# Three chained blocks on one core: the weight range check, the place of the rms gain, the first loads and the written order

## The chip, the cores and the metric

The kernel runs on one core of one Trainium2 chip. The metric is the device time of one execution in microseconds (us). The kernel before took 1032.06 us (median of 3 runs, 1030.85 to 1033.56). Engines are named as in the profile: PE is TensorE, DVE is VectorE, ACT is ScalarE, POOL is GpSimd, SP is SyncE, which issues the DMAs.

## The reference, cut to what matters

Three stages follow one another. The first is a linear recurrence over 768 positions for 4 batches of 8 heads of width 48, with complex decays normalised to a magnitude of at most 0.999. Its output becomes a matrix x of 3072 rows and 384 columns.

```python
new_re = ar * S_re - ai * S_im          # every position t, every head
new_im = ar * S_im + ai * S_re
S_re, S_im = new_re + k[t] (outer) v[t], new_im
y[t] = q[t] @ S_re
...
xn = x / rms(x) * rms_g                 # stage 2: 384 -> 1536 -> 384
x = (silu(xn @ w_gate) * (xn @ w_val)) @ w_out
h = max(x @ w1, x @ w2, x @ w3)         # stage 3: 384 -> 768 -> 384
out = h @ w_out2
```

The weights and `rms_g` arrive as 64-bit floats; the kernel reads them as pairs of 32-bit words.

## The kernel before, in words

**Two versions, one flag.** `fast` computes everything under assumptions about the ranges of the data; `ok_flag` (from line 1324) tests the assumptions, and `general` runs afterwards only if a test fails. With the inputs here only `fast` runs.

**Precision.** Every weight and every activation of stages 2 and 3 is split into two 16-bit floats, high and low, and a product is three matmuls: high by high, high by low, low by high (`mm3`, lines 1134 to 1137).

**Streams.** The work is cut into named steps. `x0` to `x11` are twelve pieces of the recurrence (two batches by 128 positions each): loads, squares (`sq0`, `sq1`), minima (`m20`, `m21`), logarithm and norm, a scan of 7 levels on DVE (`scan1x` to `scan7z`), small complex products (`pre`), the scaled q and k (`pa`, `qh`, `kr`, `kh`), transposes on PE (`tq`, `tk`), score products (`qk`), a triangular mask on POOL (`msk`), value products (`pv`), the state update (`kv`, `wa`, `wd`, `wu`), the row norm (`rs`), and the transposed, split result: `yt` on PE, then `xh` and `xl` into the tiles XH and XL. `m0` to `m5` are six blocks of 512 rows of stages 2 and 3: gate and value products (`g`, `v`), `silu`, `gate`, the split `uh`, `ul`, the product with `w_out` (`acc`, `last`), `fh`, `fl`, then stage 3: `h00` to `h52`, maxima (`mx`), split (`hh`, `hl`), `om` and the store (`ob`, `od`). Blocks 0 and 1 do stage 2 in two pieces of 256 rows (`m0`, `m0b`, `m1`, `m1b`); the others in one piece.

**Weights.** `c0` to `c59` turn the 64-bit weights into the pairs: 60 tiles of 128 by 384, each with a load (384 KB on SP's queue, three buffers), `low` on ACT (line 427), `join` and `sign` on DVE (lines 432, 436), `high` (a scaled cast, line 440) and `rest`, the remainder. For the first 24 tiles (`BYPE`) the remainder is made on PE (`dif`, lines 444 and 445: the tile times a scaled diagonal matrix `down`, minus the high part) and cast from there; for the other 36 it is one DVE instruction.

**Range test of the weights.** `norms` (lines 479 to 496) forms, for 16 groups of weights, the products of the high part with itself: `nmm` on PE (line 489, 180 matmuls of 128 columns in all) and `nmax` on DVE (line 493), which takes the largest entry off the diagonal into `g_w`. `ok_flag` compares `g_w` with limits. `late` loads all 60 weight tiles again near the end and reduces them to smallest and largest magnitudes per row, `g_low` and `g_top` (lines 469 and 473).

**The rms gain** is loaded to `gts` (line 388), clipped on DVE (`gcl`, line 391), and multiplied in when the transposed rows are split: `xh` does three scaled casts and `xl` three DVE instructions for each half of a piece (from lines 1016 and 1023), one per 128 columns, because the gain differs in each.

**Order.** Nothing is scheduled by a program at run time: `ORDER` is a string of 3682 step names, written out, and `emit` issues the steps in that order. Each engine takes its own instructions in that order, so the string fixes five queues. A name with `/a`, `/v` or `/p` also says which engine does that step (ACT, DVE, POOL). In the order before, 393 steps stand ahead of the first gate product of block 0 (`m0.g0`), 775 ahead of that of its second piece (`m0b.g0`), 1137 ahead of the fourth group of stage 3 of block 0 (`m0.h30`) and 1226 ahead of the first gate product of block 1 (`m1.g0`).

Of the kernel before, what the change touches and what calls it, by code (L numbers as in the profile page):

```python
# [32 lines left out]
BYPE = range(0, 24)  # L33
# [5 lines left out]
SW, SX, SU, S1, SH = 2.0 ** 10, 2.0 ** 8, 2.0, 2.0 ** 2, 2.0 ** 2  # L39
# [214 lines left out]
def fast(  # L254
# [148 lines left out]
    for f in (con, eye, off, tri, sels, diag, one, zero, ld_g, gcl):  # L403
        at("k", -20.0, f"k.{f.__name__}", f)
# [8 lines left out]
    def conv(t, dst, r, c0, src, r0):  # L413
# [25 lines left out]
        def high():  # L439
            mv(dst[0][:, r, c0:c0 + CW], L["c"].bitcast(F32), -SW * 2.0 ** -128)  # L440

        def dif():
# [4 lines left out]
        def rest():
# [31 lines left out]
    def norms(t, dst, rows, c0, slot):  # L479
        n = len(jobs) - 1  # L480
        L = {}

        def nmm():
            p = pm.tile([128, 3, 128], F32, tag="m", name="nrm")
            L["p"] = p
            for j in range(3):
                w = dst[0][:, :, c0 + 128 * j:c0 + 128 * j + 128]
                for r in range(rows):
                    nc.tensor.matmul(p[:, j, :], lhsT=w[:, r, :], rhs=w[:, r, :], start=(r == 0), stop=(r == rows - 1))

        def nmax():
            junk = xp.tile([128, 3, 128], F32, tag="junk", name="junk")
            nc.vector.tensor_tensor_reduce(out=junk, in0=L["p"], in1=offd.to_broadcast([128, 3, 128]), scale=1.0,  # L493
                                           scalar=-1e30, op0=ALU.add, op1=ALU.max, accum_out=g_w[:, slot:slot + 1])
        at("c", t(n + 3.0), f"n{slot}.nmm", nmm)
        at("c", t(n + 3.0), f"n{slot}.nmax", nmax)

# [1208 lines left out]
```

## Time and profile before

| | |
|---|---|
| runs before | 1030.85, 1032.06, 1033.56 us |
| profiled execution | 1028.46 us, its span 1026.7 us |
| mean granted TensorE clock | 0.983 of full speed |
| PE busy | 956.3 us, 93% of the span |
| DVE busy | 818.5 us, 80% |
| ACT busy | 478.0 us, 47% |
| POOL busy | 66.6 us, 6% |
| HBM traffic | 70.78 MB read, 4.72 MB written |

The span runs from the first to the last instruction; the execution's time is 1.8 us longer. "Busy" for PE is the union of matmuls whose ends are modelled, so it is an upper view of the work. Times inside the profile are counted from the start of the span.

### The profile page before, as it was taken

Reading aid. Unit: us, or ns where it says so; the run is one execution under the profiler, and the core shown is the slowest. Engines: PE = TensorE matmul, PEld = TensorE weight load, DVE = VectorE, ACT = ScalarE, POOL = GpSimd, SP = SyncE. Lnnn points to the kernel's source line nnn. Section 1 sums busy time; section 2 is a strip of 40 time slices with the busy share of each in tenths; the row PEclk is TensorE's granted clock in tenths of the full one; section 3 lists DMA queues with packets and bytes.
Section 4 is the critical chain, followed back from the end, with each engine's and each line's share of the span. In section 5 each row is a group of like instructions: output and inputs, shape, how many; then the busy total and the mean of one; then the engine's idle time right before and its main releaser. Section 6 shows DMA issues by size and latency. Waiting matters only on the chain.

```text
span 1026.7 us, 17237 instructions
## 1 busy us (share of the span) xinstructions
PE 956.3 (93%) x6409; PEld 602.0 (59%) x6409; DVE 818.5 (80%) x2025; ACT 478.0 (47%) x939; POOL 66.6 (6%) x67
## 2 busy tenths in 40 slices
PE   2686898998999999999999999999999999999997
PEld 1364776855688975654655555656455555544443
DVE  5999999997965899849889568998648899985261
ACT  5677677764562565514563325474225351211100
POOL 1010030021000011000101000101001000000000
PEclk9888998999999999999999999999999999999999
DMA  7464563641321133121221131213011426682001
GB/s 193 144 174 116 137 181 92 189 124 27 69 72 28 38 69 70 39 53 49 51 51 34 22 74 44 51 44 77 1 45 52 116 87 193 212 279 78 1 1 34
DMA packets 84652, 87.52 MB, mean 85 GB/s; under 512 B 51920, under 2 KB 69200, under 8 KB 84560
## 3 DMA queue, kind: packets, MB, share of 16 engines
q1 hardware_dynamic: 84560, 86.34, 30.9%
q8 instruction: 52, 0.85, 0.3%
q14 instruction: 40, 0.33, 0.1%
HBM read 70.78 MB, written 4.72 MB: 74 GB/s over the span
## 4 chain that ended last, share of the span: by engine, by line
PE 62%; DVE 10%; DMA 2%; ACT 2%; issue 2%; POOL 1%; SPq 1%; DVEq 0%; ACTq 0%; POOLq 0%
PE gv L1135 7%; PE gv L1136 7%; PE gv L1137 7%; PE hm L1135 5%; PE hm L1136 5%; PE hm L1137 5%; PE acc L1135 3%; PE acc L1136 3%; PE acc L1137 3%; PE yp L897 3%; PE tp L838 2%; PE qk L862 2%; PE om L1289 2%; PE om L1291 2%; PE om L1290 2%; PE kp L943 2%
## 5 line engine op out<-in xcount | busy, mean ns | idle before, releaser
L880 POOL TENSOR_SCALAR_AFFINE_SELECT P<-P 128x512 f32<-128x512 f32 x48 | 62.1, 1304 | 794.1 <-ACT P L332 739.4
L1135 PE MATMUL gv<-XH,wgh 128*128 128x256 f16 (+1 forms) x288 | 94.5, 328 | 3.5 <-DVE g_w L493 1.9
L1135 PE MATMUL gv<-XH,wvh 128*128 128x256 f16 (+1 forms) x288 | 94.7, 329 | 3.2 <-ACT sg L1163 3.2
L1136 PE MATMUL gv<-XL,wgh 128*128 128x256 f16 (+1 forms) x288 | 94.4, 328 | 1.9 <-DVE XL L267 1.9
L1137 PE MATMUL gv<-XH,wgl 128*128 128x256 f16 (+1 forms) x288 | 94.4, 328 | 1.1 <-DVE wgl L267 1.1
L1137 PE MATMUL acc<-uh,wol 128*128 128x256 f16 (+1 forms) x288 | 93.8, 326 | 1.0 <-DVE wol L267 1.0
L1137 PE MATMUL gv<-XH,wvl 128*128 128x256 f16 (+1 forms) x288 | 94.7, 329 | 0.0
L1136 PE MATMUL gv<-XL,wvh 128*128 128x256 f16 (+1 forms) x288 | 94.7, 329 | 0.0
L1135 PE MATMUL acc<-uh,woh 128*128 128x256 f16 (+1 forms) x288 | 93.9, 326 | 0.0
L1136 PE MATMUL acc<-ul,woh 128*128 128x256 f16 (+1 forms) x288 | 93.8, 326 | 0.0
L1163 ACT ACTIVATE sg<-gv 128x256 f32<-128x256 f32 (+1 forms) x96 | 46.4, 489 | 84.3 <-PE gv L1137 71.8
L267 DVE SCALAR_TENSOR_TENSOR sg<-gv,sg 128x256 f32<-128x256 f32 (+1 forms) x96 | 52.8, 552 | 33.0 <-PE gv L1137 31.8
L267 DVE SCALAR_TENSOR_TENSOR hs<-hm,hs 128x512 f32<-128x512 f32 x72 | 49.4, 687 | 31.7 <-PE hm L1137 31.2
L343 DVE TENSOR_TENSOR ul<-sg,uh 128x256 f16<-128x256 f32 (+1 forms) x96 | 53.2, 559 | 14.5 <-ACT uh L332 13.9
L332 ACT CAST uh<-sg 128x256 f16<-128x256 f32 (+1 forms) x74 | 36.3, 495 | 57.9 <-DVE sg L267 35.3
L862 PEld LDWEIGHTS qk<-qT,kT 96*128 96x128 f32 x384 | 48.4, 196 | 3.9 <-issue 0.8
L862 PE MATMUL qk<-qT,kT 96*128 96x128 f32 x384 | 50.3, 281 | 0.0
L1289 PE MATMUL om<-uoh,HH 128*128 128x384 f16 x144 | 47.0, 326 | 0.0
L1291 PE MATMUL om<-uoh,HL 128*128 128x384 f16 x144 | 46.9, 326 | 0.0
L1290 PE MATMUL om<-uol,HH 128*128 128x384 f16 x144 | 46.9, 326 | 0.0
L354 ACT ACT_TABLE_LOAD x34 | 43.6, 1283 | 1.4 <-PEq L1690 0.8
L897 PE MATMUL yp<-P,v 128*64 128x128 f32 x384 | 35.8, 275 | 7.6 <-POOL P L880 7.5
(231 smaller groups left out, 2322.0 us busy)
## 6 DMA issues: line engine op xcount, KB each, us to landing
kn<-KH SPq DMA_DIRECT2D x160, 48.0 KB
raw<-in_moe_w_out_dram SPq DMA_DIRECT2D x18, 384.0 KB
raw<-in_moe_w_dram SPq DMA_DIRECT2D x18, 384.0 KB
lw<-in_moe_w_out_dram SPq DMA_DIRECT2D x18, 384.0 KB
lw<-in_moe_w_dram SPq DMA_DIRECT2D x18, 384.0 KB
ar<-in_a_re_dram SPq DMA_DIRECT2D x24, 192.0 KB
ai<-in_a_im_dram SPq DMA_DIRECT2D x24, 192.0 KB
raw<-in_moe_w_gate_dram SPq DMA_DIRECT2D x12, 384.0 KB
```

The lines of the kernel that those rows point to most:

```text
L267: nc.vector.scalar_tensor_tensor(out=o, in0=a, scalar=s, in1=b, op0=op0, op1=op1)
L343: eng[on(opts)].tensor_tensor(out=o, in0=a, in1=b, op=op)
L862: nc.tensor.matmul(p[:, j, :], lhsT=kT[:, h, :], rhs=qT[0:96, h, :], start=True, stop=True)
L880: nc.gpsimd.affine_select(out=P, in_=P, pattern=[[0, 4], [1, TP], [TP, TQ]], base=0, channel_multiplier=-1, compare_op=ALU.is_ge, fill=0.0)
L897: nc.tensor.matmul(L["y", jb][64 * z:64 * z + 64, 2 * g + pair, :], lhsT=(vt if part else Wf)[:, c:c + 64], rhs=P[:, 2 * pair + z, :] if p ...
L1135: nc.tensor.matmul(o, lhsT=wh, rhs=xh, start=first, stop=False)
L1136: nc.tensor.matmul(o, lhsT=wh, rhs=xl, start=False, stop=False)
L1137: nc.tensor.matmul(o, lhsT=wl, rhs=xh, start=False, stop=last)
L1163: nc.scalar.activation(s, L.pop(("g", j)), AF.Silu, scale=1.0 / (SW * SX))
L1289: nc.tensor.matmul(p, lhsT=hh[:, j, ts], rhs=WO2[0][:, j, :], start=(j == 0), stop=False)
L1290: nc.tensor.matmul(p, lhsT=hh[:, j, ts], rhs=WO2[1][:, j, :], start=False, stop=False)
L1291: nc.tensor.matmul(p, lhsT=hl[:, j, ts], rhs=WO2[0][:, j, :], start=False, stop=(j == NJ2 - 1))
```

## The change

The test by products goes; in its place `ok_flag` derives bounds from the row maxima that `late` already gathers. The gain `rms_g` is multiplied into the rows of `w_gate` and `w_val` when they are converted (`gsc` holds gain times scale, and `down` becomes one diagonal per group of 128 rows), so `xh` and `xl` become one instruction each on 384 columns. The first `ai` load is issued from ACT's queue beside `ar` on SP's. The 24 tiles whose remainder is made on PE are now the gate and value tiles among the first 36. The constants `offd` and `mask` go. Two power-of-two scales change (SU, SH). The order is written anew: 3649 steps, with 36 activation-table changes where there were 34; 349 steps stand ahead of `m0.g0`, 745 ahead of `m0b.g0`, 1078 ahead of `m0.h30` and 1186 ahead of `m1.g0`. The 16 `nmm` and 16 `nmax` are gone from it.

```diff
-BYPE = range(0, 24)
+BYPE = [n for n in range(36) if n % 9 < 6]
...
     def diag():
-        nc.scalar.mul(down, ident, -SW * 2.0 ** -128)
+        for kt in range(KT):
+            nc.scalar.mul(down[:, kt], ident, gsc[:, kt:kt + 1])
         nc.scalar.mul(less, ident, -1.0)
...
     def gcl():
         nc.vector.tensor_scalar(out=gts, in0=gts, scalar1=5.9, scalar2=-5.9, op0=ALU.min, op1=ALU.max)
+        nc.vector.tensor_scalar(out=gsc, in0=gts, scalar1=-SW * 2.0 ** -128, scalar2=None, op0=ALU.mult)
...
+        by = gsc[:, r:r + 1] if gain else -SW * 2.0 ** -128
...
         def high():
-            mv(dst[0][:, r, c0:c0 + CW], L["c"].bitcast(F32), -SW * 2.0 ** -128)
+            mv(dst[0][:, r, c0:c0 + CW], L["c"].bitcast(F32), by)
...
-    def norms(t, dst, rows, c0, slot):
...
-                    nc.sync.dma_start(out=t[:, jb].rearrange("p t d -> p (t d)"),
+                    dma = nc.scalar if n == 0 and nm == "ai" else nc.sync
+                    dma.dma_start(out=t[:, jb].rearrange("p t d -> p (t d)"),
...
         def xh(jb):
-                for kk in range(KT):
-                    mv(XH[:, kk, c0:c0 + 128], L["yT", jb][:, kk], gts[:, kk:kk + 1])
+                mv(XH[:, :, c0:c0 + 128], L["yT", jb])
...
         def xl(jb):
-                for kk in range(KT):
-                    stt(XL[:, kk, c0:c0 + 128], L["yT", jb][:, kk], gts[:, kk:kk + 1], XH[:, kk, c0:c0 + 128],
-                        ALU.mult, ALU.subtract)
+                tt(XL[:, :, c0:c0 + 128], L.pop(("yT", jb)), XH[:, :, c0:c0 + 128], ALU.subtract)
...
     def ok_flag():
-        ge(o[4], g_w, 0.5 * SW * SW)
-        tt(o[5], g_w, lim, ALU.is_le)
...
+        nc.vector.memset(ones, 1.0)
+        t = top[:, :NW]
+        nc.vector.tensor_scalar(out=t.bitcast(I32), in0=g_top.bitcast(I32), scalar1=3, scalar2=None,
+                                op0=ALU.logical_shift_left)
+        nc.vector.tensor_scalar(out=t, in0=t, scalar1=-2.0 ** -128, scalar2=None, op0=ALU.mult)
+        ge(o[8], t, 2.0 ** -6)
+        tt(t, t, t, ALU.mult)
+        p = pat.tile([128, NW // 3, 3], F32, tag="p", name="pn")
+        nc.tensor.matmul(p.rearrange("p t r -> p (t r)"), lhsT=ones, rhs=t, start=True, stop=True)
+        nc.vector.tensor_reduce(out=o[9], in_=p, axis=mybir.AxisListType.X, op=ALU.add)
+        le(o[9], o[9], 12.0)
...
 ORDER = """
-k.con k.eye x0.ld_ar k.one k.diag k.zero k.sels x0.ld_ai c0.load c4.load c2.load k.tri x0.ld_v0 k.off x0.ld_q x0.sq0/a
-x0.ld_k x0.ld_v1 x0.sq1/a k.ld_g x0.m21 x0.m20 c0.low c0.join x0.ln c0.sign c0.high/v c0.dif c1.load c4.low x0.nt0
...
+k.con x0.ld_ai k.eye x0.ld_ar k.tab k.one k.zero k.sels c0.load c14.load c10.load x0.ld_v0 k.ld_g x0.sq1/v x0.ld_k
+x0.ld_v1 x0.ld_q x0.sq0/a x0.m20 x0.m21 c0.low x0.ln c0.join c0.sign c4.load c14.low x0.nt0 c14.join c14.sign c10.low
...
```

In the new order, between `m0b.g0` and `m1.g0`, the last conversions come before most of `x3`'s scan, and eight of `x3`'s wide products (`pa`, `qh`) and its `n21` and last `pre` steps, which stood ahead of `m1.g0`, stand behind it.

## Rows read from the trace of the kernel before

**Rows 1.** The page, part 1: busy time, share of span, instructions.
```profile
PE 956.3 (93%) x6409; PEld 602.0 (59%) x6409; DVE 818.5 (80%) x2025; ACT 478.0 (47%) x939; POOL 66.6 (6%) x67
```
**Rows 2.** Windows: stretch, length, busy of PE, PEld, DVE, ACT, POOL; clock, DMA share, GB/s.
```profile
86.50:160.20 73.70, 60.79 (x558) 51.10 (x558) 71.00 (x196) 54.47 (x123) 8.15 (x4) 0.98 0.46 129
160.20:204.60 44.40, 41.56 (x368) 36.22 (x368) 43.77 (x101) 32.43 (x68) 0.00 (x0) 0.93 0.50 146
204.60:243.40 38.80, 33.57 (x233) 21.22 (x233) 33.71 (x75) 20.76 (x42) 9.24 (x4) 0.96 0.36 93
243.40:263.40 20.00, 19.83 (x100) 9.59 (x99) 19.42 (x65) 11.34 (x25) 0.00 (x0) 1.00 0.08 19
263.40:1019.30 755.90, 748.00 (x4880) 452.06 (x4877) 578.55 (x1394) 299.49 (x560) 40.32 (x36) 1.00 0.26 68
```
**Rows 3.** Timeline of PE at m0b.g0, m0.h30 and m1.g0: start, length, instruction.
```profile
160.21 0.37 PE L1135 MATMUL gv<-XH,wgh 128*128 128x256 f16 x1 [0.46 <-ACT XH L334]
...
162.19 0.42 PE L1135 MATMUL gv<-XH,wgh 128*128 128x256 f16 x1
...
243.44 0.38 PE L1135 MATMUL hm<-X1H,u0h 128*128 128x512 f16 x1
...
263.39 0.27 PE L1135 MATMUL gv<-XH,wgh 128*128 128x256 f16 x1
```
**Rows 4.** Windows of tile nrm alone: stretch, length, PE and DVE busy; clock, DMA.
```profile
0.00:243.40 243.40, 10.77 (x135) 6.59 (x12) 0.94 0.52 144
243.40:1027.00 783.60, 2.84 (x45) 2.20 (x4) 1.00 0.25 67
```
**Rows 5.** Groups by form: nmax, XL, XH, one 384-column cast, one 768-column product.
```profile
L493 DVE CUSTOM_DVE_ANT_1 junk<-nrm,offd 128x384 f32<-128x384 f32 x16 | 8.8, 550 | 0.1
L267 DVE SCALAR_TENSOR_TENSOR XL<-yT,gts,XH 128x128 f16<-128x128 f32 x72 | 20.2, 344 | 6.7 <-ACT XH L334 6.7
L334 ACT ACTIVATE XH<-yT,gts 128x128 f16<-128x128 f32 x60 | 17.1, 373 | 10.7 <-PE yT L1012 10.6
L332 ACT CAST wgl<-dif 128x384 f16<-128x384 f32 x9 | 4.3, 476 | 2.8 <-PE dif L445 2.7
L343 DVE TENSOR_TENSOR QH<-AA,q 128x768 f32<-128x768 f32 x24 | 22.4, 950 | 0.0
```
**Rows 6.** Timeline of DVE: two instructions that do not wait for each other.
```profile
26.05 0.35 DVE L264 TENSOR_TENSOR m<-AA 128x192 f32<-128x192 f32 x1
26.32 0.35 DVE L264 TENSOR_TENSOR m<-AA,ar 128x192 f32<-128x192 f32 x1
```
**Rows 7.** Timeline of the opening, all engines.
```profile
0.81 1.47 SPq L561 DMA_DIRECT2D ar<-in_a_re_dram  x2
2.33 1.24 SPq L561 DMA_DIRECT2D ai<-in_a_im_dram  x2
5.81 0.84 ACT L348 ACTIVATE Zn<-ar 128x768 f32<-128x768 f32 x1 [2.48 <-DMA ar<-in_a_re_dram]
9.32 0.84 ACT L348 ACTIVATE Rn<-ai 128x768 f32<-128x768 f32 x1 [2.67 <-DMA ai<-in_a_im_dram]
10.19 0.56 DVE L586 CUSTOM_DVE_ANT_0 Zn<-Zn,Rn 128x384 f32<-128x384 f32 x1 [9.22 <-ACT Rn L348]
11.99 1.30 SPq L388 DMA_DIRECT2D gts<-in_moe_rms_g_dram  x1
20.71 0.16 DVE L391 TENSOR_SCALAR gts<-gts 128x3 f32<-128x3 f32 x1
```
**Rows 8.** Timeline near the flag: the transpose of its minimum.
```profile
993.78 0.27 PE L1355 MATMUL pf<-ident,lo 128*1 128x128 f32 x1 [0.78 <-DVE lo L1353]
```
**Rows 9.** Waits of DVE, 200 to 260 us: the longest one.
```profile
DVE uol L267 <- ACT uoh L334: 4.8, 1, 4.8
```
**Rows 10.** Windows again: two stretches with both engines nearly full.
```profile
154.00:180.00 26.00, 21.52 (x183) 17.86 (x181) 25.32 (x75) 20.22 (x44) 0.00 (x0) 0.87 0.33 93
359.00:411.00 52.00, 48.62 (x398) 34.98 (x397) 49.57 (x125) 31.12 (x62) 9.29 (x6) 1.00 0.34 70
```

More of the change, by code (lines that the diff above doesn't have):

```diff
@@ L401, in zero @@
             nc.gpsimd.memset(z[96:128], 0.0)
-    for f in (con, eye, off, tri, sels, diag, one, zero, ld_g, gcl):
+    for f in (con, tab, eye, sels, ld_g, gcl, diag, one, zero):
         at("k", -20.0, f"k.{f.__name__}", f)
@@ L477, in late @@
             at("l", t, f"l{n}.{f.__name__}", f)
-    def norms(t, dst, rows, c0, slot):
[L480 to L496, printed above, removed]
     def ctime(n):
@@ L1444 @@
-c28.rest c32.load c24.high/a m0.gate8 x1.tq00 x1.ck01/a x2.ai x1.cq00/a c24.rest m0.acc6 m0.uh8/a x2.aim m0.ul8
-x1.qk01 x3.ld_ai x2.ain/a x2.ar c27.low x1.qk00 n5.nmax x2.ar0/a x1.qkc01/a c27.join c31.low x2.scan1x x1.tq10
-x1.msk01 c27.sign x1.qkc00/a c31.join x1.cq10/a c25.load x1.tq11 x1.msk00 x2.scan1y c32.low c31.sign x1.tk10
-c27.high/a x2.scan1z c33.load c31.high/a x2.scan2x n6.nmm c27.rest x1.ck10/a m0.g9 c31.rest x1.cq11/a c32.join
-x3.sq1/a x1.tk11 x2.scan2y c32.sign x1.pv00 x1.ck11/a x2.scan2z c26.load x1.pv01 n6.nmax c32.high/a n7.nmm x2.scan3y
@@ L1474 @@
-m0b.ul9 m0b.g11 c52.sign m0b.gate10 c51.load c52.high/a c56.join m0b.v11 m0b.uh10/a c52.rest m0b.silu11 m0b.ul10
-m0b.acc8 m0b.gate11 c53.low c56.sign m0b.acc9 c53.join c48.load m0b.uh11/a c56.high/a x1.wu1z m0b.acc10 m0b.ul11
-c56.rest c51.low c53.sign m0b.last0 c51.join m0b.last2 c46.load c53.high/a x2.pw x1.msm c51.sign m0b.fh0/a m0b.fh2/a
-m0b.last1 m0b.fl0 c45.load c51.high/a n9.nmm m0b.fl2 c48.low c53.rest n10.nmm m0b.fh1/a c51.rest n13.nmm x2.t12
-m0b.fl1 c48.join n10.nmax x2.rc c48.sign m0.h00 n9.nmax c59.load n13.nmax c48.high/a x2.kr0x c46.low x2.kr1x m0.h01
@@ new lines @@
+x0.ld_v1 x0.ld_q x0.sq0/a x0.m20 x0.m21 c0.low x0.ln c0.join c0.sign c4.load c14.low x0.nt0 c14.join c14.sign c10.low
+x0.nt1 c9.load k.gcl x0.nu c0.high/a c14.high/a x0.nt2/a k.diag x0.ai c0.dif x0.aim c10.join c14.dif x0.ain/a x1.ld_ai
+x0.ar c0.rest/a c10.sign x0.ar0/a x0.scan1y c14.rest/a c2.load x0.scan1x c10.high/a c10.dif x0.scan1z x0.scan2x
+x0.scan2y c10.rest/v x0.scan2z c4.low x0.scan3y x0.scan3x c4.join x0.scan3z c4.sign c9.low x0.scan4y c5.load x0.scan4x
+c4.high/a c4.dif c9.join x0.scan4z c9.sign x0.scan5y c9.high/a c3.load c9.dif x0.scan5x c4.rest/a x0.scan5z x1.sq1/a
@@ new lines @@
+x1.tk11 m0.gate8 x1.pw c28.low x2.scan5x x2.scan5y m0.uh8/a c28.join x1.ck11/a m0.ul8 x1.t12 x1.pv00 x2.scan5z
+c28.sign x1.pv01 x2.scan6y c28.high/a x1.qk10 c31.load x2.scan6x x1.yu0/a x2.scan6z c28.dif x2.scan7x x3.sq1/a
+x2.scan7y x3.ld_ar x2.scan7z x1.qkc10/a x1.yb0 c27.low x2.pt x1.msk10 x1.yc0/a c27.join x2.ptc x1.qk11 c27.sign
+c29.low x2.pre0x c32.load x1.pv10 x2.pre0y c27.high/a c29.join c27.dif x1.qkc11/a x2.pre1x c29.sign x1.ssq0/a x1.kv0
+x1.msk11 x2.pre1y c31.low c25.load x2.pre2x c27.rest/a x2.pre2y x2.pre2z c31.join c29.high/a c29.dif x2.pre3x
@@ new lines @@
+c54.sign m0b.fh0/a m0b.last2 c52.low m0b.fl0 c45.load m0b.fh1/a c52.join m0b.fh2/a c54.high/a m0b.fl1 m0b.fl2 m0.h00
+c59.low c52.sign c54.rest c52.high/a c56.load m0.h01 c59.join m0.mx00/a c52.rest c59.sign c45.low c57.load m0.h02
+c59.high/a c45.join m0.mx01 c59.rest c56.low c45.sign m0.h10 m0.mx02 c45.high/a c58.load c56.join c45.rest c57.low
+c56.sign m0.h11 m0.mx10/a c57.join c46.load c56.high/a c57.sign c56.rest c57.high/a c47.load m0.h12 c57.rest c58.low
+m0.mx11 c58.join c58.sign m0.h20 x2.rc m0.mx12 c58.high/v c58.rest x3.ln m0.h21 x2.kr0x x2.kr1x x2.kr0y x2.kr1y
@@ new lines @@
+c47.low x2.kr0z m0.h22 c46.low x2.kr1z x2.kh0 x3.ld_k x2.kh1 x2.tk00 x2.kn0 c47.join x2.ck00/a x2.tk01 c46.join
+x2.ck01/a c47.sign x3.nt0 x2.qk01 c46.sign c47.high/a x3.nt1 x2.qk00 x2.qkc01/a c46.high/v x2.msk01 x3.nu x2.tk10
+x2.qkc00/a x2.ck10/a x2.tk11 c46.rest x2.msk00 x3.nt2/v x2.kn1 x2.pv00 x2.ck11/a c47.rest swap m0.hh0/a x3.ai m0.hh1/a
+x2.pv01 m0.hl0 x2.tq10 x3.ar x2.yu0/a x2.cq10/a x2.tq11 x3.aim x2.yb0 x2.cq11/a m0.hl1 x2.yc0/a x2.kv0 x3.ain/a
+m0.big0 x4.ld_ai x2.ssq0/a x3.ar0/v x2.qk10 x3.scan1y m0.mx20/a x3.scan1x x3.ld_v0 x2.wa0 m0.h30 x3.scan1z x2.wd0
```

576 lines of the change are left out of this document (273 added, 303 removed).

## The prediction, made before the result was known

> **What bounds the kernel now.** I read the busy shares first: PE 93%, DVE 80% [rows 1]. An average over a kernel with two regimes says little, so the windows come next, and in them I looked for which engine has no idle time [rows 2]. From 86.5 to 204.6 us DVE is busy 71.00 of 73.7 and 43.77 of 44.4 us, PE 60.79 and 41.56: VectorE sets the pace, because it converts the weights beside three pieces of the recurrence. From 263.4 us to the last product PE is busy 748.0 of 755.9 us and DVE only 578.55: TensorE sets it. Between 204.6 and 263.4 one hands over to the other. So the time is: the opening, plus the DVE work that stands ahead of the hand-over in the order, plus the PE work that stands behind it, plus small waits. I take `m1.g0`, at 263.39 us [rows 3], as the marker; 763.3 us lie behind it (1026.7 less 263.4). All other waits named in the profile (ACT, POOL) are of engines that neither bounds.
>
> How DVE work is counted: an instruction of a queue that is full costs its length less about 0.08 us, since the next starts before it ends (0.35 us long, 0.27 apart [rows 6]). I went down both orders to the marker and summed by kind of step. Only the differences matter.
>
> **Part 1, the norm products go.** DVE loses 12 `nmax` ahead of the marker, 6.59 us busy by their windows [rows 4]; at 0.55 less 0.08 and the read-out behind each, 12 x 0.53 = 6.4 us. The four others (2.20 us) lie where DVE has slack: nothing. PE loses 10.77 us ahead of 243.4, where DVE sets the pace: nothing by themselves, and 2.84 us behind it, where PE is full: a whole gain.
>
> **Part 2, one `xh` and one `xl`.** Three XL instructions of 0.344 [rows 5] cost 3 x 0.26 = 0.78 us. One on 384 columns is not in the trace; a 384-column DVE instruction that reads PSUM is the `nmax`, 0.55, so 0.47 net and 0.31 us saved. Bounds: net 0.26 (as for 128 columns) to 0.78 (no gain). For the six pairs ahead of the marker 1.9 us, between 0 and 3.1; the 18 pairs behind it fall where DVE has slack. `xh`: three of 0.373 on ACT become one like the 384-column cast, 0.476: 24 x 0.6 = 15 us of ACT, on an engine 47% busy: nothing; if ACT were the late one, it would be a further gain.
>
> **Part 3, engine changes in the new order.** Counting the suffixes ahead of the marker, DVE takes over two squares, two `cq`, one `qkc`, two `ys`, two `uh`, one `high`, one `rest`, one `ar0` (from 0.88 us for a 768-column square, a width that takes 0.95 [rows 5], down to 0.13) and gives up a `yc`: together 5.0 us more. What it frees on ACT is covered.
>
> **Part 4, moved steps.** Eight 768-column products of `x3` (`pa`, `qh`; 0.950 less 0.08 each [rows 5], 7.0 us) and 1.2 us of its small steps go behind the marker, where DVE has 177 us of slack in all (755.9 less 578.55 [rows 2]); three `wu` and one `hl` come ahead, 2.0 us. Cost if that cover fails is the same 6 us. On PE two `tq` and one `pb`, about 1.1 us, go behind the marker and count there. SP's queue: its loads are reordered, but each conversion's load still finds its buffer freed by the third load before it, 4 us of DVE work or more ahead of its use but for one at 2 us, and the order before has tighter ones; I charge nothing. Two more table changes on ACT: covered.
>
> **Sum to here.** DVE ahead of the marker: -6.4 -1.9 +5.0 -8.2 +2.0 = -9.5 us. PE behind it: -2.84 +1.1 = -1.7 us. Together -11.2. The same count at `m0.h30` (243.44 us [rows 3]) gives -11.3 for DVE and +1.1 for PE, -10.2, because other steps are moved past that point. I take -10.5.
>
> **Part 5, the opening.** The first DVE work of size starts at 10.19 us, after `ai`'s square; `ar` is there at 5.81, `ai` at 9.32 [rows 7]. In the new order both are issued in parallel and squared on two engines. Bounds: nothing (the data moves no sooner) and 3.5 us (`ai` as early as `ar`). The two share the engines, so I put `ai` at about 7.6, the middle, and the square of `sq1` on DVE costs 0.1 more: -2.0 us after rounding up for the square that no longer waits behind another on ACT. [...] The new `diag` and every gate or val `high` wait for the gain. Its load is issued some eight issues earlier than now (11.99 us, used at 20.71 without a wait [rows 7]), `gcl` stands behind about 4 us of DVE work, at 12 to 13 us, so nothing; at worst, if landing takes the whole 8.7 us from issue to use, 1 to 2 us once. Four small casts for `diag` instead of two on ACT and the dropped POOL constants: covered by ACT's 2.5 us of waiting for `ar`.
>
> **Part 6, the flag.** PE now waits 0.78 us for the minimum [rows 8]. The new flag adds a product with a matrix of ones in PE's queue, and a DVE sum, a comparison and the minimum between it and the old transpose, so PE, with block 5's products queued behind, waits a second time. Bounds: 0 and 2.5; about 0.3 for the product and 1.0 for the hand-over back, so +1.3 us.
>
> **Result.** -10.5 -2.0 +1.3 = -11.2 us on a span of 1026.7. The profiled execution (1028.46) lies 3.6 us under the median of the runs; from the median, 1032.06 - 11.2 = **1021 us**.
>
> **Rivals.** (a) *The wait inside the hand-over goes as well.* In 200 to 260 us DVE waits 4.8 us once, for a cast behind a queue of ACT [rows 9]. In the new order the last conversions stand ahead of the late score copies that ACT was held by. If nothing takes its place: 1032.06 - 11.2 - 4.8 = 1016, with the full 3.5 us in the opening 1015. For: the order at that place; against: PE's new work between `h22` and `h30` is a chain of transposes, scores and masks with almost no other product between, so a similar wait can sit there.
>
> (b) *Lockstep.* In the new order PE's and DVE's work from `m0b.g0` to `m1.g0` are nearly equal (85 and 87 us, before 88 and 96). Two full in-order queues that feed each other lose time on both. In 359 to 411 us, where both are nearly full, PE idles 3.4 of 52 us [rows 10]; on 85 us that is 6 us more. 1027; with no gain in the opening 1029, and the change is not worth telling from noise. About 3 us, 0.3%, is what a measurement of this kernel can tell from none.
>
> (c) *Slower: the idle share of 154 to 180 us becomes the rule.* There DVE is full and PE idles 4.5 of 26 us, 17% [rows 10]. From `m0b.g0` to block 1's `h00`, the new order has 203 us of PE work and 194 of DVE, where the old had 201 and 182, so DVE is late more easily right after the marker. Before, PE idles 8.2 us from 160.2 to the marker [rows 2] and 3.4 more by the end of block 1's gate products [rows 10], 12 in all; at 17% it would idle 42, 30 more: 1051. It decides once some 23 us, 10% of the stretch, are lost. Speaking against: in 263 to 1019 us PE idles 7.9 us in all [rows 2]. [...]
>
> (d) *The second queue does nothing* for `ai`: 1023; it is inside the range of the forecast and changes no sign.
>
> **How the numbers follow.** Forecast with its bounds (1016 to 1028): 0.55. (a), below 1016: 0.14. (b), 1029 to 1035: 0.15. (c), above 1035: 0.16. Faster by over 0.3% (under 1029): 0.69; within 0.3%: 0.15; slower: 0.16. Range: the low end is (a) with the full opening and 4 us off the small waits, 1011; the high end is (b) plus the flag's upper bound and a late gain, 1033, which leaves most of (c) outside.
>
> **What would show each step.** The rows of `nrm` gone; XL and XH in 24 instructions each, near 0.55 and 0.48; the first DVE minimum at about 8 us instead of 10.19; `m0.h30` near 231 and `m1.g0` near 252 us; DVE full until about 230 us; PE idle of about 8 us from there to the last product; a second PE wait near the flag of about 1 us. The prediction is wrong if `m1.g0` comes at 260 or later (the DVE count or the opening failed), or if PE's idle time behind it exceeds 15 us (a new wait in the order), and wrong the other way if DVE's long wait goes and `m1.g0` comes before 248.

## The result, and the profile after

The kernel after takes **1018.78 us** (median of 4 runs, 1017.69 to 1019.02) against 1032.81 for the kernel before in the same session (4 runs): ratio 0.9863, 95% interval 0.9843 to 0.9883. That is 14.0 us less, 2.2 us under the forecast of 1021 and inside its range. The profiled execution took 1017.69 us (span 1016.0), 10.7 us less in span than that of before; the sum of the prediction was 11.2. Of these 10.7, 8.2 lie ahead of `m1.g0` and 2.5 behind it.

The page of the kernel after, part 1 [answers to rows 1]:

```profile
PE 941.9 (93%) x6231; PEld 589.8 (58%) x6231; DVE 818.4 (81%) x1966; ACT 462.5 (46%) x877; POOL 60.9 (6%) x63
```

The shares are those of before, so they say nothing of the cause. The windows between the same steps do [rows 2]; in order: `m0.g0` to `m0b.g0`, to `m0.h00`, to `m0.h30`, to `m1.g0`, to near the end.

```profile
85.65:164.19 78.54, 66.05 (x519) 51.22 (x518) 76.56 (x194) 57.56 (x121) 4.49 (x4) 0.96 0.50 136
164.19:202.07 37.88, 37.29 (x344) 33.21 (x341) 36.31 (x86) 25.48 (x63) 0.00 (x0) 1.00 0.62 179
202.07:232.78 30.71, 28.37 (x183) 16.54 (x181) 29.79 (x57) 22.48 (x41) 2.72 (x2) 1.00 0.47 118
232.78:255.21 22.43, 22.43 (x141) 11.99 (x139) 22.00 (x78) 11.10 (x22) 2.48 (x2) 1.00 0.18 50
255.21:1008.60 753.39, 746.15 (x4846) 450.56 (x4844) 584.68 (x1369) 293.32 (x526) 41.99 (x36) 1.00 0.25 69
```

`m0b.g0` comes 4.0 us later than in the profile before, `m0.h00` 2.5 earlier, `m0.h30` 10.7 earlier, `m1.g0` 8.2 earlier [rows 3]. From `m0b.g0` to `m1.g0` PE and DVE are each busy 88.1 of 91.0 us: the two are nearly full together. Behind the marker, up to the end of the last window, PE idles 7.2 us (7.9 before). PE's timeline at the three steps:

```profile
164.19 0.27 PE L1100 MATMUL gv<-XH,wgh 128*128 128x256 f16 x1
...
232.78 0.38 PE L1100 MATMUL hm<-X1H,u0h 128*128 128x512 f16 x1
...
255.21 0.27 PE L1100 MATMUL gv<-XH,wgh 128*128 128x256 f16 x1
```

The groups [rows 5]: `nrm` is gone, and XL and XH have the lengths that were forecast (0.55 and 0.48).

```profile
L264 DVE TENSOR_TENSOR XL<-yT,XH 128x384 f16<-128x384 f32 x24 | 12.6, 550 | 0.7 <-ACT XH L330 0.7
L330 ACT CAST XH<-yT 128x384 f16<-128x384 f32 x19 | 8.7, 477 | 2.9 <-PE yT L981 2.9
```

DVE's waits from 200 to 260 us: where before one of 4.8 us stood [rows 9], the longest is now

```profile
DVE HL L341 <- ACT HH L330: 0.5, 1, 0.5
```

The opening [rows 7] went the other way than forecast: the first minimum starts at 12.11 us, not at 8, and not at 10.19 as before.

```profile
0.82 1.86 ACTq L533 DMA_DIRECT2D ai<-in_a_im_dram  x2
0.82 1.53 SPq L533 DMA_DIRECT2D ar<-in_a_re_dram  x2
2.40 0.45 SPq L402 DMA_DIRECT2D raw<-in_moe_w_gate_dram  x1
...
8.94 0.84 ACT L346 ACTIVATE Zn<-ar 128x768 f32<-128x768 f32 x1 [4.40 <-DMA ar<-in_a_re_dram]
...
11.00 0.96 DVE L348 TENSOR_TENSOR Rn<-ai 128x768 f32<-128x768 f32 x1 [10.01 <-DMA ai<-in_a_im_dram]
12.11 0.56 DVE L558 CUSTOM_DVE_ANT_0 Zn<-Zn,Rn 128x384 f32<-128x384 f32 x1
```

PE at the flag [rows 8]: two waits, 2.45 us lost between the product at 980.47 and the one at 983.14 (2.67 apart, less the 0.22 that stand between two products), where before it was 1.04.

```profile
980.47 0.38 PE L1102 MATMUL hm<-X1H,u1l 128*128 128x512 f16 x1
981.55 0.40 PE L1323 MATMUL pn<-top,ones 128*128 128x60 f32 x2 [0.70 <-DVE top L264]
983.03 0.27 PE L1329 MATMUL pf<-ident,lo 128*1 128x128 f32 x1 [1.07 <-DVE lo L1327]
983.14 0.38 PE L1100 MATMUL hm<-X1H,u2h 128*128 128x512 f16 x1
```

So the number came out, and one term had the wrong sign. The experiments ask whether the other terms were right.

### The profile page after: what moved, and what is told of

Its sections match the earlier page's. It is cut to its first block, busy times and chain, and to the rows that moved or that the text cites. A ratio compares the mean times of both kernels' runs of the same rounds, so it can differ in the third digit from the quotient of the medians.

```text
span 1016.0 us, 16755 instructions
## 1 busy us (share of the span) xinstructions
PE 941.9 (93%) x6231; PEld 589.8 (58%) x6231; DVE 818.4 (81%) x1966; ACT 462.5 (46%) x877; POOL 60.9 (6%) x63
## 4 chain that ended last, share of the span: by engine, by line
PE 71%; DVE 7%; ACT 1%; issue 1%; POOL 1%; DVEq 0%; ACTq 0%
PE gv L1100 7%; PE gv L1101 7%; PE gv L1102 7%; PE hm L1100 7%; PE hm L1101 7%; PE hm L1102 7%; PE yp L866 3%; PE acc L1100 3%; PE acc L1102 3%; PE acc L1101 3%; PE tp L810 3%; PE qk L834 3%; PE om L1254 2%; PE om L1256 2%; PE om L1255 2%; PE kp L912 2%
## 5 line engine op out<-in xcount | busy, mean ns | idle before, releaser
L849 POOL TENSOR_SCALAR_AFFINE_SELECT P<-P 128x512 f32<-128x512 f32 x48 | 57.4, 1205 | 780.1 <-ACT P L330 543.7
L330 ACT CAST uh<-sg 128x256 f16<-128x256 f32 (+1 forms) x67 | 33.2, 498 | 54.5 <-DVE sg L267 48.5
L438 PE MATMUL dif<-cvc,down 128*128 128x384 f32 x48 | 27.2, 656 | 26.5 <-ACT down L375 20.2
L834 PE MATMUL qk<-qT,kT 96*128 96x128 f32 x384 | 49.3, 279 | 0.9 <-ACT kT L330 0.7
L330 ACT CAST HH<-hs 128x512 f16<-128x512 f32 x25 | 15.4, 619 | 71.1 <-DVE hs L267 71.1
```

The lines of the kernel that those rows point to most:

```text
L330: nc.scalar.copy(o, i)
L834: nc.tensor.matmul(p[:, j, :], lhsT=kT[:, h, :], rhs=qT[0:96, h, :], start=True, stop=True)
L849: nc.gpsimd.affine_select(out=P, in_=P, pattern=[[0, 4], [1, TP], [TP, TQ]], base=0, channel_multiplier=-1, compare_op=ALU.is_ge, fill=0.0)
```

## The experiments

All twelve in one table. Times are medians. Ratios go to runs of the kernel before beside them and use all runs, so they can differ a little from what two medians give (e3: 0.9960 by the medians). The last three columns are from each profiled execution: when `m1.g0` starts, DVE's busy time up to there (one window) and the difference, its idle time. One thing has to be known to read them: the profiled execution of before (1028.46) is 4 us below its median. Three later kernels with the same order up to 215 us or more (e5, e9, f1) have `m0.h00` at 207.8 to 208.0 us, not at 204.59; about 267 is the usual place of `m1.g0` before. The profiled executions of h_new_old (1037.34) and f3 (1020.73) are 4.9 and 6.8 us above their medians, so their `m1.g0` is later than usual.

| kernel | us | ratio, interval | `m1.g0` | DVE busy | DVE idle |
|---|---|---|---|---|---|
| before | 1032.81 | | 263.39 | 239.99 | 23.4 |
| e5 (before, one cast moved) | 1034.52 | 1.0008, 0.9987 to 1.0030 | 267.46 | 240.04 | 27.4 |
| e9 (before, one square moved) | 1033.61 | 1.0010, 0.9991 to 1.0029 | 266.63 | 240.24 | 26.4 |
| f1 (before, score chain moved) | 1034.23 | 1.0016, 0.9998 to 1.0033 | 270.11 | 240.14 | 30.0 |
| e3 (before, no norms) | 1028.57 | 0.9973, 0.9947 to 0.9999 | 265.55 | 235.63 | 29.9 |
| e4 (new code, old order) | 1030.68 | 0.9972, 0.9948 to 0.9996 | 264.11 | 235.75 | 28.4 |
| h_old_new | 1025.06 | 0.9934, 0.9910 to 0.9958 | 261.20 | 232.22 | 29.0 |
| h_new_old | 1032.49 | 1.0010, 0.9991 to 1.0030 | 270.21 | 237.24 | 33.0 |
| **after** | 1018.78 | 0.9863, 0.9843 to 0.9883 | 255.21 | 233.76 | 21.5 |
| e8 (after, 16 steps back on ACT) | 1020.40 | 0.9870, 0.9829 to 0.9912 | 259.78 | 228.97 | 30.8 |
| f2 (after, `m0.h30` later) | 1020.36 | 0.9885, 0.9863 to 0.9906 | 256.02 | 233.24 | 22.8 |
| d_pad (after, 12 more on DVE) | 1023.99 | 0.9908, 0.9891 to 0.9925 | 261.99 | 239.25 | 22.7 |
| e1 (after, one queue) | 1017.40 | 0.9854, 0.9828 to 0.9880 | 254.20 | 233.59 | 20.6 |
| f3 (after, one queue, flag cut) | 1013.91 | 0.9814, 0.9793 to 0.9836 | 260.12 | 232.42 | 27.7 |

### What the code is worth without the order: e3 and e4

e3 takes the norm products out of the kernel before.

```diff
-            norms(ctime, w, KT, g * CW, 2 * g + s)
...
-        ge(o[4], g_w, 0.5 * SW * SW)
-        tt(o[5], g_w, lim, ALU.is_le)
```

> The kernel before without the norm products, their maxima, their mask and their two comparisons in the flag; the rest of its code and order stays. The theory of the prediction (DVE's work ahead of the hand-over plus PE's behind it): 12 maxima are 6.4 us of DVE ahead of m1.g0 and PE's 45 products behind 243 us are 2.84, so m1.g0 comes 6.4 us earlier than in the kernel before and the time is 9 us lower, about 1023.5. Rival: the places of the maxima are filled by waits for ACT and PE that stand there anyway, and only the 2.84 us of PE count: about 1030, m1.g0 moves by less than 2 us.

Measured: 0.27% (2.8 us, by the interval 0.1 to 5.5; 4.1 by the medians), well under the 9.2 of the count. DVE is 4.4 us less busy ahead of `m1.g0` than in e5, and 2.5 us more idle; `m1.g0` moves by 1.9. Its longest waits from 200 to 262 us:

```profile
DVE uol L267 <- ACT uoh L334: 5.2, 1, 5.2
DVE KH L267 <- ACT KH L794: 1.4, 1, 1.4
```

The 4.8 us wait [rows 9] has grown to 5.2 and a second has come beside it. The rival is the nearer one. That the gain is PE's 2.84 us alone is not separated: behind `m1.g0` the profile of e3 has 761.8 us, and the four with the code of before (before, e5, e9, f1) 762.8 to 766.0.

e4 is the new code in the old order, with the first loads on one queue and with the old choice of the 24 tiles whose remainder PE makes (the diagonal for the 6 `w_out` tiles among them is one more constant).

```diff
-BYPE = [n for n in range(36) if n % 9 < 6]
+BYPE = range(0, 24)
...
-                    dma = nc.scalar if n == 0 and nm == "ai" else nc.sync
+                    dma = nc.sync
```

> The code after in the order before (all loads on SP's queue, the gain's load and the diagonals put ahead of the first conversion; the 24 tiles whose remainder PE makes are those of before; norm steps left out). By the counts the code changes alone are worth 6.4 + 2.84 (norms) + 1.9 (XL) less 1.4 (flag), about 9.7 us: 1023; the new order by the counts is then worth nothing (+5.0 -8.2 +2.0 +1.1) but the 4.8 us wait of DVE in the hand-over, which stays in this kernel. So theory one: about 1023, DVE waits some 5 us for uoh between 225 and 235 us. Rival: the order is the gain and the code is hidden: 1028 or more. Second rival: the order is worth nothing, the wait moves with the rest: 1019.

Measured: 0.28% (2.9 us, 0.4 to 5.4), no more than e3: XL, XH and the gain in the weights give nothing that these runs can tell beside the flag's extra cost. The first rival holds: from e4's ratio to that of after, 1.1% or 11 us, is the order (with the second queue and the other choice of the 24 tiles in it). At `m1.g0` the two profiles differ by 8.9 us, of which DVE's busy time is 2.0 and its idle time 6.9; another 4.5 us lie behind `m1.g0`. The windows of e4 from `m0.g0` to `m0b.g0` and from `m0.h00` to `m0.h30` tell where the idle time is:

```profile
86.62:163.30 76.68, 62.23 (x496) 50.71 (x495) 70.62 (x183) 54.17 (x119) 5.46 (x4) 0.88 0.46 129
205.05:244.88 39.83, 34.14 (x235) 20.54 (x233) 35.86 (x77) 23.57 (x47) 3.98 (x4) 0.96 0.40 109
```

DVE idles 6.1 and 4.0 us in them, and 2.0 and 0.9 in the same two of the kernel after. The larger part of the difference, 4.1 us, lies ahead of the hand-over, where none of the runs that move a single step (e5, e9, f2) looks. And the wait of some 5 us for `uoh` that theory one expected is not in e4: DVE's longest between `m0.h00` and `m0.h30` is 1.4 us.

### What DVE's work is worth in the new order: d_pad and e8

```diff
+    def pad(i, t, dst, r, c0):
+        def f():
+            junk = xp.tile([128, CW], F32, tag="junk", name="junk")
+            w = dst[0][:, r, c0:c0 + CW]
+            nc.vector.tensor_tensor(out=junk, in0=w, in1=w, op=ALU.mult)
```

> The kernel after with 12 extra instructions on DVE, each a product of 384 columns of a finished weight tile into a tile that nobody reads, about where the 12 maxima of the norm products stood in the order before (8 ahead of m0b.g0, all ahead of m0.h00); no products on PE. It measures what DVE work ahead of the hand-over is worth in the new order: the 12 come to 12 x 0.47 = 5.6 us of DVE's queue. The theory of the prediction (a full DVE queue, time is its count): m1.g0 comes 5 to 6 us later, at 260 to 261, time 1023.5 to 1025. Rival, after the run without norm products, where as much work less gave 1 to 2 us at m1.g0: half of the stretch's idle time or more takes it up, m1.g0 at 256 to 257.5, time 1019.5 to 1021.5.

Measured: +5.2 us by the medians (4.6 by the ratios), for 12 instructions of 0.55 us, 5.6 with the overlap taken off. DVE's busy time grows by 5.5 and its idle time by 1.3; the idle time is not evenly spread, for between `m0.g0` and `m0b.g0` DVE waits 3.0 us for ACT once (0.9 in after), and a mask there takes 5.69 us. In the new order the rule of the prediction, a full queue costs its length, fits the measured time; in the old order, by e3, it doesn't. The two are not mirror images: e3 takes out maxima that read PSUM, with their products on PE, and d_pad adds products that read SBUF. That the kind of work and not the order makes the difference is not excluded.

e8 hands 16 steps back to ACT.

```diff
-x0.sq1/v
+x0.sq1/a
...
-x1.cq01/v
+x1.cq01/a
```

> The kernel after with 16 steps ahead of m1.g0 given back from DVE to ACT, as in the order before (the squares x0.sq1 and x2.sq1, two cq, one qkc, two ys, two uh, two ar0, three casts high, two remainders). The prediction charged DVE about 5 us for such swaps and called ACT's part covered. If both hold, DVE has 6 to 7 us less ahead of m1.g0, which comes at about 249, and the time is about 1013. Rival: ACT is the late one at these places, so DVE and PE wait for it there and the swaps were no cost: m1.g0 at 254 to 257, time 1017 to 1021.

Measured: 0.9870 against 0.9863, no difference that four runs can tell. DVE loses 4.8 us of work and gains 9.4 of idle time, 1.5 of it up to `x0.pt` and 3.4 between `m0.h00` and `m0.h30`, where its two longest waits are for ACT:

```profile
DVE m L264 <- ACT AA L330: 1.6, 1, 1.6
DVE uol L267 <- ACT uoh L332: 1.1, 1, 1.1
```

In the kernel after no wait of DVE there is over 0.3 us. With those steps on ACT, ACT is late. The rival holds: the forecast of 1013 is outside the interval, and the swaps were no cost that shows.

### Where in the order: two halves, and one step

h_old_new is the code of e4 with the order before up to `m0.h00` and the rest in the order after. h_new_old is the code after, second queue included, with the reverse.

> The code after (first loads on one queue) with the order before up to m0.h00 and all that is left in the order after. The four runs before this one said that the code alone is worth 0.3% and DVE's count little; the gain of the new order is made between m0.h00 and m0.h30 (39.8 us in the old order with the new code, 30.7 in the kernel after). New theory: what ends late there is x2's score chain, held because ACT, in order, waits for the load of x4's ai (x4.sq1) with x2's score copies behind it; the new order has that square elsewhere. Then this kernel has the gain: 31 to 33 us from m0.h00 to m0.h30, time 1018 to 1022. Rival: the gain is prepared ahead of m0.h00 (steps of x2 and conversions done earlier there), and this kernel stays at 1027 or more.

> The counterpart: the kernel after with its own order up to m0.h00 and the order before behind it. New theory: the stretch m0.h00 to m0.h30 is long again, 38 us or more, and the time is 1027 to 1031. Rival (prepared ahead): 1018 to 1022.

Measured: against e4, the new second half alone is worth 0.4%, the new first half alone is a loss of 0.4%, and both together 1.1% (each of these differences is known to about 0.3%). From `m0.h00` to `m0.h30` it is 35.4 us in h_old_new, not 31 to 33, and 49.3 in the late execution of h_new_old that was profiled. Neither half has the gain: my theory (all in the second half, by a square that waits for its load) and its rival (all in the first) both fall. A written order of five queues is worth what its parts are worth together.

f2 moves a single step of the new order.

```diff
-x2.wa0 m0.h30 x3.scan1z x2.wd0 x2.qkc10/v x3.scan2x x2.msk10 x3.scan2y m0.mx21 x2.qk11 x3.scan2z m0.mx22 x2.pv10
+x2.wa0 x3.scan1z x2.wd0 x2.qkc10/v x3.scan2x x2.msk10 x3.scan2y m0.mx21 x2.qk11 x3.scan2z m0.mx22 x2.pv10 m0.h30
...
```

> The kernel after with one step moved: m0.h30 stands behind x2.qk11 and x2.pv10 in PE's queue, as in the order before. Theory now: PE then waits at pv10 for the copy and the mask with no product to do, 2 to 4 us, and since TensorE sets the pace from m0.h00 on in this kernel, the wait reaches the end: m1.g0 at 257 to 259, time 1020.5 to 1023. Rival: DVE sets the pace up to m1.g0 (it is busy 22.0 of the 22.4 us behind m0.h30), PE catches up, and m1.g0 stays at 255, the time at 1018 to 1019.5.

Measured: `m0.h30` comes 2.8 us later but `m1.g0` only 0.8 (counted from `m0.h00`, 3.4 and 1.4); the time is 1020.36, between the two forecasts, and its interval overlaps that of after. PE catches up most of it behind `m0.h30`.

### The wait inside the hand-over: e5, e9, f1 and the mask

Three attempts to take the 4.8 us wait out of the kernel before by its order alone:

```diff
-c47.sign m0.h22 x3.scan7y x2.qkc11/a x3.scan7x c57.rest c47.high/a x4.ld_ar
+c47.sign c47.high/a m0.h22 x3.scan7y x2.qkc11/a x3.scan7x c57.rest x4.ld_ar
...
```

> The kernel before with one step moved: the cast c47.high on ACT now stands ahead of the three products m0.h22 and of the score copy x2.qkc11 that held ACT for 6.75 us. If that queue on ACT alone made DVE's 4.8 us wait, the wait goes and m1.g0 and the end come up to 4.8 us earlier: about 1028. Rival: PE waits 3.6 us in the same place for the mask on POOL, and PE and DVE reach m1.g0 by the scores anyway: DVE's wait moves to the next maxima behind PE and the time stays at 1031 to 1033.

e9 moves `x4.sq1/a` from ahead of `x2.qk10` to just ahead of `x4.sq0/a`.

> The kernel before with one step moved: the square x4.sq1 on ACT, which waits 1.2 to 3.7 us for its load in these traces, stands behind x2's score copies, next to x4.sq0. New theory: the copies, the mask on POOL and PE's product come earlier by that wait and the square, 2 to 4 us; PE's wait of 3.6 us for the mask falls under 1.5, m0.h30 comes 2 to 4 us earlier after m0.h00 than before, the time is 1029 to 1030.5. Rival: the mask waits for the scores themselves (transposes and PE's place in the order), and nothing moves: 1032 to 1034.

```diff
-x2.msk10 x3.scan5z c58.rest x2.pv10 x3.scan6y x3.scan6x c47.join x2.qk11 x3.scan6z c47.sign m0.h22 x3.scan7y x2.qkc11/a
+x2.msk10 x3.scan5z c58.rest x3.scan6y x3.scan6x c47.join x3.scan6z c47.sign m0.h22 x2.pv10 x2.qk11 x3.scan7y
+c57.rest c47.high/a c47.rest swap m0.hh0/a m0.hh1/a x2.qkc11/a
...
```

> The kernel before, mended in one place of its order between m0.h20 and m0.h30: PE's products x2.pv10 and x2.qk11, which wait for the mask on POOL, go behind m0.h22; the last casts c47.high, c47.rest and m0.hh0, m0.hh1 go ahead of the score copy x2.qkc11. Theory now: in the order before, x2's second score chain (copy on ACT, mask of 4.2 us on POOL, pv10, qk11, copy) stands in all the queues ahead of m0.h30, each engine waits for it in turn, and moving one step only hands the wait on (e5, e9). Then this move of both, on PE and on ACT, takes PE's 3.6 us wait down to about 1.5 and DVE's 4.8 to 5.4 us wait mostly away: from m0.h00 to m0.h30 some 36 us instead of 39, time 2 to 4 us lower, 1028 to 1030. Rival: the stretch is set by the conversions' loads and DVE's count, and the time stays at 1031 to 1034.

All three: no gain (one execution of e9 took 3053 us; it is left out and not explained). DVE's longest wait of each, in the order e5, e9, f1:

```profile
DVE HL L343 <- ACT HH L332: 5.4, 1, 5.4
```

```profile
DVE uol L267 <- ACT uoh L334: 4.5, 1, 4.5
```

```profile
DVE m L264 <- ACT Tn L674: 4.9, 1, 4.9
```

The wait stays and only changes its name. What the three have in common stands one row further back, in POOL's timeline of the kernel before: two equal masks of 512 columns.

```profile
230.05 4.17 POOL L880 TENSOR_SCALAR_AFFINE_SELECT P<-P 128x512 f32<-128x512 f32 x1 [8.44 <-ACT P L332]
237.89 0.84 POOL L880 TENSOR_SCALAR_AFFINE_SELECT P<-P 128x512 f32<-128x512 f32 x1 [3.68 <-ACT P L332]
```

And DVE's timeline beside them:

```profile
232.69 0.54 DVE L267 SCALAR_TENSOR_TENSOR uol<-cvc,uoh 128x384 f16<-128x384 f32 x1
233.16 0.34 DVE L264 TENSOR_TENSOR AA<-m,m 128x192 f32<-128x192 f32 x1
238.28 0.83 DVE L267 SCALAR_TENSOR_TENSOR uol<-cvc,uoh 128x384 f16<-128x384 f32 x1 [4.77 <-ACT uoh L334]
```

The second mask, begun while DVE is idle, takes 0.84 us. The first one takes 4.17: it stands beside ten DVE instructions with two inputs in SBUF that follow each other without a gap from 229.94 us on, and it ends 0.7 us after DVE's queue has run dry at 233.50. Then the chain unrolls: PE, which waited 3.6 us for the mask, does its products, ACT's copy follows, then the cast behind it on ACT, and only then DVE goes on. Read so, DVE waits, through POOL, PE and ACT, for a mask that took 4.17 us beside its own instructions, where the next, begun behind them, took 0.84. In the profiles of before and after, the 11 masks beside which DVE ran no instruction with two inputs in SBUF took 0.84 to 0.85 us each; every longer one stood beside at least one such instruction. In e5, e9 and f1 that mask takes 4.18, 4.25 and 4.49 us: nothing that I moved touched it. In the kernel after, the masks of this piece take 1.64, 1.12, 1.17 and 1.30. Over the whole kernel, masks of more than 3 us number five each in before, e5, e9 and f1, three in e3 and h_new_old, two in e4, one in f3 and d_pad, and none in h_old_new, after, e8, f2 and e1. Between `m0.h00` and `m0.h30` a mask takes over 3 us in seven of the fourteen profiles (before, e3, e5, e9, f1, h_new_old, f3), and in these DVE's longest wait there is 4.5 to 8.2 us. In the other seven no mask there takes over 1.7 us, and DVE's longest wait is 0.3 to 1.8 us.

The sharpest pair is e1 and f3, whose instructions in this stretch are the same in the same order. In e1's profile, POOL and DVE:

```profile
222.84 2.71 POOL L849 TENSOR_SCALAR_AFFINE_SELECT P<-P 128x512 f32<-128x512 f32 x2 [84.70 <-ACT P L330]
```

```profile
222.82 0.95 DVE L267 SCALAR_TENSOR_TENSOR Rn<-AA,Rn 128x768 f32<-128x768 f32 x1
223.69 1.16 DVE L267 SCALAR_TENSOR_TENSOR uol<-cvc,uoh 128x384 f16<-128x384 f32 x1
224.77 1.19 DVE L591 TENSOR_SCALAR AA<-Rn 128x768 f32<-128x768 f32 x1
225.89 0.54 DVE L267 SCALAR_TENSOR_TENSOR uol<-cvc,uoh 128x384 f16<-128x384 f32 x1
```

In f3's:

```profile
221.71 8.26 POOL L849 TENSOR_SCALAR_AFFINE_SELECT P<-P 128x512 f32<-128x512 f32 x2 [83.59 <-ACT P L330]
```

```profile
221.69 0.95 DVE L267 SCALAR_TENSOR_TENSOR Rn<-AA,Rn 128x768 f32<-128x768 f32 x1
...
227.78 0.68 DVE L1243 CUSTOM_DVE_ANT_0 junk<-X1H 128x512 f32<-128x512 f16 x1
228.39 0.07 DVE L1243 DVE_READ_ACCUMULATOR2_ANT g_x<- 128x1 f32 x1
236.66 0.21 DVE L336 COPY AA<-ar 128x96 f32<-128x96 f32 x1 [8.19 <-ACT AA L332]
```

In both the first mask begins 0.02 us after the same DVE instruction (`Rn`). In e1 the two masks took 1.63 and 1.12 us, and two DVE instructions beside them took 0.6 us more than their forms (1.16 and 1.19 where these take 0.54 and 0.55). In f3 the first mask took 7.46 us of the 8.26: DVE's instructions followed each other without a gap until it ran dry at 228.46, the mask ended 0.7 us later, and DVE then waited 8.2 us. From `m0.h00` to `m0.h30` it is 31.3 us in e1 and 37.7 in f3; f3's profiled execution took 1020.73 us, its five others 1012.67 to 1015.41. So masks of one form took 7.46 us beside DVE's unbroken row in f3, 1.63 beside the same instructions in e1, and 0.84 in before while DVE was idle as it began; what makes one of them longer than another, these rows do not show. That the long mask is the cause of DVE's long wait is read from fourteen profiles; moving the mask to another engine, or breaking up DVE's row beside it, was not tried. Nor is this wait what makes the old order slow: in e4 the mask takes 0.86 us at this place, the long wait is gone, and from `m0.h00` to `m0.h30` it is still 39.8 us (38.9 in before, 41.5 in e3).

### The opening: e1

```diff
-                    dma = nc.scalar if n == 0 and nm == "ai" else nc.sync
+                    dma = nc.sync
```

> The kernel after with both first loads on SP's queue, ai ahead of ar. In the profile after, the first minimum on DVE starts at 12.11 us, before at 10.19. Theory one: the second queue makes both loads late (they share the DMA engines with each other and with the raw loads behind them); with one queue the first minimum is back at 10.2 to 10.4, and the time 0 to 2 us lower, 1017 to 1019. Rival: the code of the opening before also gave 11.6 us in two later profiles, so the start varies from execution to execution, and this kernel may land anywhere from 10.2 to 12.2, with the time at 1018 to 1020.

```profile
5.75 0.96 DVE L348 TENSOR_TENSOR Rn<-ai 128x768 f32<-128x768 f32 x1 [4.77 <-DMA ai<-in_a_im_dram]
9.35 0.84 ACT L346 ACTIVATE Zn<-ar 128x768 f32<-128x768 f32 x1 [6.70 <-DMA ar<-in_a_re_dram]
10.22 0.56 DVE L558 CUSTOM_DVE_ANT_0 Zn<-Zn,Rn 128x384 f32<-128x384 f32 x1 [3.52 <-ACT Zn L346]
```

The first minimum is back at 10.22. At `x0.pt` 1.9 us of that are still there (30.99 against 32.88), at `m1.g0` 1.0, and the time, 1.4 us lower in the medians, cannot be told from that of after. One profile isn't enough here. Nine have one queue (before, e1, e3, e4, e5, e9, f1, f3, h_old_new): the first load is used at 5.7 to 6.1 us in all of them, the first minimum starts at 10.19 to 11.69, median 10.78. Five have two queues (after, e8, f2, d_pad, h_new_old): the first load is used at 7.3 to 8.9 us (10.7 in e8, which squares `ai` first), the first minimum starts at 11.48 to 12.48, median 12.11. So theory one holds in its effect, at 1.3 us between the medians. The 16 DMA engines are as full with one queue as with two: from 6 to 8 us their mean busy share is 1.07 in before and 1.05 in after; that sharing them makes the loads late was not shown. And the rival is right that one execution differs from the next by as much.

### The flag cut in four steps: f3

One queue as in e1, and `ok` cut in four steps:

```diff
-m5.fl2 m5.h00
+m5.fl2 okt m5.h00
...
-m5.h11
+m5.h11 okp
...
-m5.big2 ok m5.h32
+m5.big2 okr m5.h32 okf
```

> The kernel after with both first loads on SP's queue and the flag cut in four steps: the scaled maxima on DVE ahead of m5.h10, the product with ones behind m5.h11, the comparisons and the minimum behind m5.big2, the transpose of the minimum behind m5.h32. In the kernel after PE loses 2.45 us between the last product ahead of the flag and the first behind it, of which 0.4 us are its two products. If only the waits cost, 2.0 us go, and the time is about 1.5 to 2 us under that of the kernel with one queue alone (1017.4): 1015.5. Rival: the end of this stretch is not PE's queue but the stores and DVE, and nothing moves: 1017 to 1018.

PE's timeline at the two products of the flag:

```profile
973.50 0.38 PE L1102 MATMUL hm<-X1H,u1l 128*128 128x512 f16 x1
973.71 0.33 PE L1316 MATMUL pn<-top,ones 128*128 128x60 f32 x2
973.88 0.38 PE L1100 MATMUL hm<-X1H,u2h 128*128 128x512 f16 x1
...
987.26 0.38 PE L1102 MATMUL hm<-X1H,u2l 128*128 128x512 f16 x1
987.48 0.27 PE L1338 MATMUL pf<-ident,lo 128*1 128x128 f32 x1
987.59 0.38 PE L1100 MATMUL hm<-X1H,u0h 128*128 128x512 f16 x1
```

Neither waits: 0.17 and 0.11 us for the two. From `m5.h00` to `m5.h32` it is 21.59 us, in e1 23.87. The median is 1013.91, ratio 0.9814 (0.9793 to 0.9836), 4.9 us under the kernel after and 3.5 under e1, somewhat more than the 2.3 us that the two profiles show. Its interval lies wholly below that of after and just overlaps that of e1.

## Why the prediction was right, and where its steps failed

**The number was right by luck: two errors cancel.** By the terms of the prediction the code was worth 9.8 us (6.4 + 2.84 + 1.9 less 1.3 for the flag), the order about nothing and the second queue 2.0. The runs give 2.9 us for the code (e4) and about 11 for the order with the second queue and the other choice of tiles. The step that failed is in the first part: "So the time is: the opening, plus the DVE work that stands ahead of the hand-over in the order", with "Only the differences matter". In the order before DVE is idle 23 to 30 us ahead of the marker, 11 to 13 of them up to `x0.pt`, and of what e3 takes off its queue (4.4 us) more than half (2.5) comes back as idle time. So a count of DVE's work does not give the time there.

- Part 1: -6.4 (DVE) and -2.84 (PE) were charged; e3 measures 2.8 for both together (at most 5.5), which is about the term for PE; the two were not measured apart, but the term for DVE does not fit beside it.
- Part 2: lengths right (0.55 and 0.48), the gain of 1.9 not seen (e4 is no faster than e3, with the flag's 1.4 against it).
- Part 3: +5.0 for work that DVE takes over. e8 gives as much back (4.8 us) and gains nothing; "What it frees on ACT is covered" was wrong, ACT was late there.
- Part 4: with part 3 the order came to about nothing (+5.0 -8.2 +2.0 +1.1). By e4 and after it is worth 11 us. What it brings is for the most part not a smaller count but less idle time: 6.9 of the 8.9 us at `m1.g0`. Which of the moved steps save it stays open; neither half of the order does alone. That `m0.h30` and `m1.g0` came near the forecast (232.78 and 255.21 for 231 and 252) was no proof of the count.
- Part 5: -2.0, and it is a loss at the first minimum, 1.3 us between the medians of the profiles. Both ends of the bound (0 and 3.5) excluded a loss, without a reason that did so. The profiles show no gain. Here `ai`'s two issues took 1.86 us on ACT, and the raw loads entered SP's queue 1.2 us earlier (2.40 for 3.61) beside the first loads. Which of the two makes the loads late was not tried. The gain's load cost nothing that PE or DVE waited for where they set the pace.
- Part 6: +1.3 forecast, +1.4 measured (2.45 less 1.04), in two waits as described.

**The rivals.** (a) happened in its effect: the 4.8 us wait went, and no wait over 0.5 us took its place, but the time did not go under 1016, because the count that it was to come on top of did not hold. Its reason, "a cast behind a queue of ACT", was one link of the chain; e5 moved that cast and gained nothing. (b) did not: PE and DVE are both nearly full from `m0b.g0` to `m1.g0`, and each idles only 2.9 us. (c) did not: PE idles 2.9 us from `m0b.g0` to the marker and 7.2 in all behind it, not 42, and the granted clock is 1.00 in every window there. (d) was nearest for the second queue, which did less than nothing.

A run that would have told the count's fault before the change was made is e3: one part of the change alone, in the old order.

## What to carry to other kernels

An engine at 97% in a window (DVE from 86.5 to 204.6 us before) is not yet the one that sets the pace: before pricing work by its count, add or remove a known amount of it (d_pad: 5.2 us for 5.6; e3: 2.8 for 9.2). Where several in-order queues feed each other, moving one step of a chain passed the wait on here (5.4, 4.5 and 4.9 us in e5, e9 and f1 for 4.8 in before); look for the link whose own length changes from row to row. A mask on POOL that reads SBUF had no fixed length here, 0.84 us begun beside an idle DVE and up to 7.46 beside a long row of DVE instructions with two inputs in SBUF; keep such a step off a chain that others wait for. And a wait that goes (e4) need not bring its length: look what the stretch as a whole does.

## What was not expected of the hardware

- The same mask of 128 by 512 on POOL took from 0.84 to 7.46 us (f3, the first of its two). Of the 672 masks in the fourteen profiles 30 took over 3 us. The five in before each stood beside a row of DVE instructions that followed each other almost without a gap, and ended 0.70 to 0.71 us after the last one of it with two inputs in SBUF that took no longer than its form does.
- The same instructions in the same order took 31.3 and 37.7 us between `m0.h00` and `m0.h30` (e1, f3). With the mask begun at the same place, two DVE instructions took 0.6 us more than their forms in one execution (e1), and the mask 5.8 us more in the other (f3, 7.46 for 1.63).
- Two loads issued at once from two queues were both used later than the first of two from one queue (7.3 us at best against 5.7 to 6.1).
